# Two batches of attention with float32 products, unnormalised weights and a divisor from ones beside v

## The chip, the core and the metric

The kernel runs on one core of a Trainium2 chip. The core has a matrix engine (TensorE, in the profile PE, with its weight loads as PEld), a vector engine (VectorE, DVE), a scalar engine (ScalarE, ACT), GpSimd (POOL) and SyncE (SP), whose queue starts all transfers here. [...] The metric is the device time of one execution in microseconds, taken as the median of several runs.

## What is computed

```python
# q, k, v: (8 batches, 8 heads, 576 positions, 64)
scores = (q @ k.transpose) / sqrt(64)
mask   = (i // 64) >= (j // 64)          # block causal
scores = where(mask, scores, -1e9) - max(scores)
attn   = exp(scores); attn = attn / (sum(attn) + 1e-9)
x      = (attn @ v), heads side by side: (4608 tokens, 512)
h      = x @ w_in                         # (512, 2048)
g      = h if h >= 1, 0 if h <= -1, else (h + 1)**2 / 4
out    = g @ w_out                        # (2048, 512)
```

All inputs and the output are float32.

## The kernel before

Attention is worked pair by pair: a pair is two heads of one batch, so there are 32 pairs, four to a batch (`Pair`, numbered b and hp). The 576 positions of a head are four full tiles of 128 rows and a last block of 64; the last blocks of both heads share a tile. `attention_steps` walks through the pairs in eight steps each (between two `yield`), and the steps of neighbouring pairs overlap: while pair `cur` is in its first two steps, the products with v of the pair before, `old`, are finished, and in the later steps q and k of the next pair, `nxt`, are loaded, split and transposed.

For each group of rows `scores` makes the scores on PE, their negated maximum on DVE (line 394) and the exponential on ACT (line 398), which also gives the sum of each row; `inverse` adds 1e-9 and takes the reciprocal of that column on DVE (lines 380, 381), and line 404 scales the rows of P in SBUF. `scores_last` does the same for the shared last tile (lines 418 to 430). `turn` and `turn_last` transpose P on PE (line 443, from pair 12 on line 441) into a PSUM bank, and `split` brings it to SBUF: `pa` for the first 256 columns, `pb` for the other 320, `pc` or `pcs` for the last block of keys.

Products in most of the kernel are made in fp32r with a high and a low half: `split` writes the high half on ACT (line 434) and the low half on DVE (line 436), `split_v` does so for v on ACT and POOL (lines 316, 317) into `vsr`, whose 128 columns are the high half in the columns of the head's own 64 and the low half in the other 64. `weighted` multiplies (line 480); its PSUM rows are then two halves to be added, which `add_halves` does through `xtmp` (ACT, line 502; DVE, line 503) into `x32`. `store_x` writes x as a high half (ACT, line 545) and a low half (POOL, line 546) to the rings `xh` and `xl`.

Batch 0 is marked `plain`. There P stays one float32 tile, and v is loaded straight into `vs`, with 64 columns of zeros beside the head's own 64; `both` adds the products of both heads in one bank and writes `xh` and `xl` itself (lines 515, 516). `vs` has one buffer and is loaded anew for each pair.

`work_bank` gives PSUM banks: it alternates between four banks of the feed-forward's output and three work banks until the feed-forward begins, and from then on gives the three alone.

The driver at the end runs the attention's steps. With each it converts pieces of the two weight matrices (`convert`: a transfer, two ACT, three DVE, a POOL, an ACT and a POOL instruction, lines 159 to 182), 64 pieces in all, and from step 36 on (`START`, the middle of pair 4) it takes one step of the feed-forward (`ffn_in`: 12 products a step, lines 626 to 643; `ffn_out`: 12 more, lines 650 and 655) with each step of the attention. What is left of the feed-forward follows when the attention is done. The order in which instructions stand on each engine comes from a scheduler, which starts from this order; each engine then works through its own in that order.

Of the kernel before, what the change touches and what calls it, by code (L numbers as in the profile page):

```python
# [23 lines left out]
def block_attn_then_ffn(  # L24
# [9 lines left out]
    nc = tc.nc  # L34
# [22 lines left out]
    CW = 256  # L57
    F32_TOP = float.fromhex("0x1.dffffcp-96")
    KA = D + NTL
    HOP = 3  # L60

    const = ctx.enter_context(tc.tile_pool(name="const", bufs=1))
# [167 lines left out]
        return moved  # L230


    class Pair:


# [2 lines left out]
        def __init__(self, b, hp):  # L238
            self.b, self.hp = b, hp

            self.plain = b == 0
            self.first = b == 0 and hp == 0

            self.hop = b >= HOP
            self.pr, self.nat = {}, {}

        def load(self, name):
            src = {"q": q, "k": k, "v": v}[name]
            h0 = 2 * self.hp
            if name == "v" and self.plain:  # L250

                self.vs = []
                both = att1.tile([P, 2, NTL + 1, 2, D], F32, tag="pb1", name="vs")
                for j in range(2):
                    vs = both[:, j]
                    nc.gpsimd.memset(vs[:, :, 1 - j, :], 0.0)
                    nc.sync.dma_start(
                        vs[:, :NTL, j, :], src[self.b, h0 + j, :SM, :].rearrange("(t p) d -> p t d", p=P)
                    )
                    nc.sync.dma_start(vs[:BLK, NTL, j, :], src[self.b, h0 + j, SM:, :])  # L260
                    self.vs.append(vs)
                return
            t_ = att2.tile([P, 2 * NTL + 2, D], F32, tag="nat", name=name + "n")
            if name == "v":
                for j in range(2):
                    nc.sync.dma_start(
                        t_[:, j * NTL : (j + 1) * NTL, :],
                        src[self.b, h0 + j, :SM, :].rearrange("(t p) d -> p t d", p=P),
                    )
                nc.sync.dma_start(  # L270
                    t_[:BLK, 2 * NTL :, :],
                    src[self.b, h0 : h0 + 2, SM:, :].rearrange("h p d -> p h d"),
                )
            else:

                nc.sync.dma_start(
                    t_[:, : 2 * NTL, :].rearrange("p (h t) d -> p h (t d)", h=2),
                    src[self.b, h0 : h0 + 2, :SM, :].rearrange("h (p t) d -> p h (t d)", t=NTL),
                )
                for j in range(2):  # L280
                    nc.sync.dma_start(
                        t_[j * BLK : (j + 1) * BLK, 2 * NTL, :], src[self.b, h0 + j, SM:, :]
                    )
            self.nat[name] = t_
# [76 lines left out]
        def begin_b(self):  # L361
            dt, n = (F32, 1) if self.plain else (F32R, 2)
            self.pb = [att1.tile([P, 2, NTL, G1], dt, tag=f"pb{i}", name=f"pb{i}") for i in range(n)]
            self.pc = (
                [att1.tile([BLK, 2, BLK], dt, tag="pa01", name="pc")] if self.plain else pcs
            )
            if not self.plain:
                self.x32 = att1.tile([P, S], F32, tag="x32", name="x32")

        def product(self, ps, j, c0, k0, n, first, last):  # L370
            nc.tensor.matmul(  # L371
# [11 lines left out]
        def scores(self, j, g):  # L383
            tiles = self.GROUPS[g]
            m = len(tiles)
            ps = work_bank("ps_s")
            pr = att3.tile([P, S], F32, tag="pr", name="pr")
            nm = small.tile([P, 2], F32, tag="nm", name="nm")
            sm = small.tile([P, 2], F32, tag="sm", name="sm")
            cols = [slice(at, at + (t + 1) * P) for t, at in tiles]  # L390
            for (t, _), cs in zip(tiles, cols):
                self.product(ps[:, cs], j, t * P, 0, (t + 1) * P, True, True)
            for i, cs in enumerate(cols):
                nc.vector.tensor_reduce(  # L394
                    out=nm[:, i : i + 1], in_=ps[:, cs], axis=AX.X, op=ALU.max, negate=True
                )
            for i, cs in enumerate(cols):
                nc.scalar.activation(  # L398
                    pr[:, cs], ps[:, cs], AF.Exp, bias=nm[:, i : i + 1], scale=1.0,
                    accum_out=sm[:, i : i + 1],  # L400
                )
            self.inverse(sm[:, :m])
            for i, cs in enumerate(cols):
                nc.vector.tensor_scalar_mul(pr[:, cs], pr[:, cs], sm[:, i : i + 1])  # L404
            self.pr[j, g] = as_float32r(pr[:, : cols[-1].stop]) if self.hop else [pr]

        def scores_last(self):

            half = S // 2
            pr = att3.tile([P, S], F32, tag="pr", name="pr")  # L410
            nm = small.tile([P, 3], F32, tag="nm", name="nm")
            sm = small.tile([P, 3], F32, tag="sm", name="sm")
            banks = []
            for i in range(2):
                ps = work_bank("ps_s")
                for j in range(2):
                    self.product(ps[:, :half], j, SM, i * half, half, j == 0, j == 1)
                nc.vector.tensor_reduce(
                    out=nm[:, i : i + 1], in_=ps[:, :half], axis=AX.X, op=ALU.max, negate=True
                )  # L420
                banks.append(ps)
            nc.vector.tensor_tensor(out=nm[:, 2:3], in0=nm[:, 0:1], in1=nm[:, 1:2], op=ALU.min)
            for i in range(2):
                nc.scalar.activation(
                    pr[:, i * half : (i + 1) * half], banks[i][:, :half], AF.Exp,
                    bias=nm[:, 2:3], scale=1.0, accum_out=sm[:, i : i + 1],
                )
            nc.vector.tensor_tensor(out=sm[:, 2:3], in0=sm[:, 0:1], in1=sm[:, 1:2], op=ALU.add)
            self.inverse(sm[:, 2:3])
            nc.vector.tensor_scalar_mul(pr, pr, sm[:, 2:3])  # L430
            self.pr["last"] = as_float32r(pr) if self.hop else [pr]

        def split(self, ps, hi, lo=None):
            nc.scalar.copy(hi, ps)  # L434
            if lo is not None:
                nc.vector.tensor_tensor(out=lo, in0=ps, in1=hi.bitcast(F32), op=ALU.subtract)  # L436
# [36 lines left out]
                ps[:BLK, :P].rearrange("p (h c) -> p h c", h=2), *(x[:BLK] for x in self.pc)  # L473
            )

        def weighted(self, ps, j, parts, first=True, last=True):
            for i, (kt, lo_col, mov) in enumerate(parts):
                vt = self.vs[j][: (BLK if self.plain and kt == NTL else P), kt, :, :]
                for m, x in enumerate(mov):
                    nc.tensor.matmul(  # L480
                        ps[:, lo_col:], vt, x,
                        start=first and i == 0 and m == 0,
                        stop=last and i == len(parts) - 1 and m == len(mov) - 1,
                    )

        def parts_first(self, j):
# [17 lines left out]
                out=self.x32[main, c0 : c0 + n], in0=ps[main, :], in1=xtmp[main, :n], op=ALU.add  # L504
            )

        def both(self, c0, parts):

            n = (G0, G1)[c0 > 0]
            ps = work_bank("ps_av")[:, :n]  # L510
            for j in range(2):
                self.weighted(ps, j, parts(j), j == 0, j == 1)
            at = self.b * S + c0
            hi = xh[:, self.hp, at : at + n]
            nc.scalar.copy(hi, ps)
            nc.vector.tensor_tensor(  # L516
                out=xl[:, self.hp, at : at + n], in0=ps, in1=hi.bitcast(F32), op=ALU.subtract
            )

        def attn_v_first(self):  # L520
            if self.plain:
                return self.both(0, self.parts_first)
            ps = work_bank("ps_av")
            for j in range(2):
                self.weighted(ps[:, j * G0 : (j + 1) * G0], j, self.parts_first(j))
            for j in range(2):
                self.add_halves(ps[:, j * G0 : (j + 1) * G0], j, 0)

        def attn_v(self, j):
            if self.plain:  # L530
                return self.both(G0, self.parts) if j else None
            ps = work_bank("ps_av")[:, :G1]
            self.weighted(ps, j, self.parts(j))
            self.add_halves(ps, j, G0)

        def store_x(self):

            if self.plain:
                return
            c0 = 0  # L540
            while c0 < S:
                at = (self.b * S + c0) % RING
# [9 lines left out]
    def attention_steps():  # L552
# [11 lines left out]
        for i, cur in enumerate(pairs + [None]):  # L564
            nxt = pairs[i + 1] if i + 1 < len(pairs) else None
            if cur:
                cur.scores(0, 0)
                cur.turned(False, 1)
                cur.load("v")
            if old:  # L570
                old.turn(1, 2)
            yield
# [3 lines left out]
            if old:  # L576
                old.attn_v(1)
                old.store_x()
            if not cur:
                return  # L580
            yield
# [159 lines left out]
```

## Time and profile before

| | |
|---|---|
| median of 3 runs | 1286.38 us |
| lowest, highest | 1285.29, 1288.21 us |
| the profiled execution | 1285.23 us |
| its span, first to last instruction | 1283.5 us |
| mean granted TensorE clock | 0.983 |
| HBM read, written | 120.59 MB, 17.83 MB |

A line of the profile names the line of the kernel, the engine, the operation, the tiles that it writes and reads with their shapes, the count, and then busy time, mean duration and idle time of the engine before it. Where two stretches of time are compared, a row gives the length, each engine's busy time with its count of instructions, the granted clock of TensorE (1.00 is full), and what the transfers did. Rows of a timeline give the start and the length. A wide instruction and the next on the same engine overlap a little in these records, so the busy time of an engine is less than the sum of its durations.

### The profile page before, as it was taken

Reading aid. Unit: us, or ns where it says so; the run is one execution under the profiler, and the core shown is the slowest. Engines: PE = TensorE matmul, PEld = TensorE weight load, DVE = VectorE, ACT = ScalarE, POOL = GpSimd, SP = SyncE. Lnnn points to the kernel's source line nnn. Section 1 sums busy time; section 2 is a strip of 40 time slices with the busy share of each in tenths; the row PEclk is TensorE's granted clock in tenths of the full one; section 3 lists DMA queues with packets and bytes.
Section 4 is the critical chain, followed back from the end, with each engine's and each line's share of the span. In section 5 each row is a group of like instructions: output and inputs, shape, how many; then the busy total and the mean of one; then the engine's idle time right before and its main releaser. Section 6 shows DMA issues by size and latency. Waiting matters only on the chain.

```text
span 1283.5 us, 20410 instructions
## 1 busy us (share of the span) xinstructions
PE 1207.2 (94%) x6496; PEld 1018.7 (79%) x6496; DVE 888.4 (69%) x2204; ACT 766.3 (60%) x1855; POOL 472.2 (37%) x466
## 2 busy tenths in 40 slices
PE   5877787899999999999999999999999999999998
PEld 4666665688888888888888888888888888888886
DVE  8998999877677777677777777777777767322222
ACT  6878676666666666666666666666666655322222
POOL 3545766633333333333333333333333332222222
PEclk9889999999999999999999999999999999999999
DMA  5656555434333545555444644464545443333432
GB/s 152 175 151 180 170 186 177 145 125 140 97 106 111 189 143 153 160 159 178 147 155 154 187 137 152 153 189 148 159 146 186 156 142 120 115 99 99 132 99 99
DMA packets 136812, 188.44 MB, mean 147 GB/s; under 512 B 61040, under 2 KB 87664, under 8 KB 136704
## 3 DMA queue, kind: packets, MB, share of 16 engines
q1 hardware_dynamic: 136704, 187.13, 47.2%
q8 instruction: 52, 0.85, 0.3%
q14 instruction: 56, 0.46, 0.1%
HBM read 120.59 MB, written 17.83 MB: 108 GB/s over the span
## 4 chain that ended last, share of the span: by engine, by line
PE 70%; DVE 13%; ACT 8%; issue 4%; DMA 2%; POOL 1%; SPq 1%; ACTq 0%; POOLq 0%; DVEq 0%
PE ph L626 26%; PE po L650 16%; PE po L655 8%; PE ps_av L480 7%; PE ps_s L371 3%; PE ps_s L374 3%; ACT pr L398 3%; PE ps_t L441 3%; PE ps_qk L327 2%; DVE pr L404 2%; ACT qb L331 2%; DVE nm L394 2%; DVE work L169 1%; PE ps_t L443 1%; DVE work L172 1%
## 5 line engine op out<-in xcount | busy, mean ns | idle before, releaser
L641 POOL TENSOR_TENSOR gl<-t,gh 128x512 fp32r<-128x512 f32 x144 | 187.2, 1300 | 577.5 <-ACT gh L640 310.8
L650 PE MATMUL po<-wo,gh 128*128 128x512 f32 x1152 | 299.7, 403 | 0.1
L650 PEld LDWEIGHTS po<-wo,gh 128*128 128x128 f32 x1152 | 210.6, 190 | 40.3 <-ACT gh L640 0.6
L626 PE MATMUL ph<-xh,wih 128*128 128x512 f32 x576 | 238.2, 414 | 1.7 <-DVE t L639 1.7
L636 DVE SCALAR_TENSOR_TENSOR t<-t 128x512 f32<-128x512 f32 x144 | 112.9, 784 | 183.1 <-ACT t L635 181.0
L626 PE MATMUL ph<-xl,wih 128*128 128x512 f32 x576 | 227.4, 395 | 1.1 <-DVE xl L516 1.1
L626 PE MATMUL ph<-xh,wil 128*128 128x512 f32 x576 | 227.9, 396 | 0.0
L635 ACT ACTIVATE t<-ph 128x512 f32<-128x512 f32 x144 | 86.0, 597 | 155.2 <-PE ph L626 155.2
L398 ACT ACTIVATE pr<-ps_s,nm 128x128 f32<-128x128 f32 (+3 forms) x256 | 134.2, 529 | 63.1 <-DVE nm L394 62.8
L655 PE MATMUL po<-wo,gl 128*128 128x512 f32 x576 | 155.4, 391 | 0.0
L394 DVE TENSOR_REDUCE nm<-ps_s 128x1 f32<-128x128 f32 (+3 forms) x256 | 123.6, 485 | 45.2 <-PE ps_s L374 43.6
L371 PE MATMUL ps_s<-ka,qa 68*128 68x288 f32 (+4 forms) x384 | 123.6, 336 | 20.5 <-ACT pr L398 12.8
L640 ACT CAST gh<-t 128x512 fp32r<-128x512 f32 x144 | 90.0, 625 | 84.6 <-DVE t L639 83.0
L626 PEld LDWEIGHTS ph<-xh,wil 128*128 128x128 f32 x576 | 109.4, 190 | 24.5
L434 ACT CAST pb<-ps_t 128x512 fp32r<-128x512 f32 (+1 forms) x140 | 77.5, 553 | 84.8 <-PE ps_t L441 65.5
L317 POOL TENSOR_TENSOR vsr<-vn,vsr 128x256 fp32r<-128x256 f32 (+1 forms) x112 | 82.9, 750 | 119.9 <-ACT vsr L316 119.9
L655 PEld LDWEIGHTS po<-wo,gl 128*128 128x128 f32 x576 | 108.4, 188 | 23.4
L626 PEld LDWEIGHTS ph<-xl,wih 128*128 128x128 f32 x576 | 109.9, 191 | 20.4 <-DVE xl L516 1.4
L626 PEld LDWEIGHTS ph<-xh,wih 128*128 128x128 f32 x576 | 109.4, 190 | 20.3 <-DVE t L639 2.0
L374 PE MATMUL ps_s<-kb,qb 128*128 128x288 f32 (+4 forms) x384 | 121.8, 323 | 0.0
L436 DVE TENSOR_TENSOR pb<-ps_t,pb 128x512 fp32r<-128x512 f32 (+1 forms) x140 | 88.1, 629 | 40.5 <-ACT pb L434 40.5
L404 DVE TENSOR_SCALAR pr<-pr,sm 128x128 f32<-128x128 f32 (+3 forms) x256 | 110.3, 451 | 3.6
(95 smaller groups left out, 2039.1 us busy)
## 6 DMA issues: line engine op xcount, KB each, us to landing
wo<-wo_split SPq DMA_DIRECT2D x144, 512.0 KB, 3.4
prr<-pr SPq DMA_DIRECT2D x80, 192.0 KB, 2.6
prr<-pr SPq DMA_DIRECT2D x60, 256.0 KB, 2.4
out_dram<-ob SPq DMA_DIRECT2D x36, 256.0 KB, 4.0
qn<-in_q_dram SPq DMA_DIRECT2D x32, 256.0 KB, 2.9
kn<-in_k_dram SPq DMA_DIRECT2D x32, 256.0 KB, 3.0
bits<-in_moe_w_in_dram SPq DMA_DIRECT2D x32, 256.0 KB, 3.1
bits<-in_moe_w_out_dram SPq DMA_DIRECT2D x32, 256.0 KB, 3.1
```

The source lines that it names most:

```text
L371: nc.tensor.matmul(ps, qa[:KA, j, c0 : c0 + P], ka[:KA, j, k0 : k0 + n], start=first, stop=False)
L374: nc.tensor.matmul(ps, qb[:, j, c0 : c0 + P], kb[:, j, k0 : k0 + n], start=False, stop=last)
L394: nc.vector.tensor_reduce(out=nm[:, i : i + 1], in_=ps[:, cs], axis=AX.X, op=ALU.max, negate=True)
L398: nc.scalar.activation(pr[:, cs], ps[:, cs], AF.Exp, bias=nm[:, i : i + 1], scale=1.0, accum_out=sm[:, i : i + 1],)
L404: nc.vector.tensor_scalar_mul(pr[:, cs], pr[:, cs], sm[:, i : i + 1])
L480: nc.tensor.matmul(ps[:, lo_col:], vt, x, start=first and i == 0 and m == 0, stop=last and i == len(parts) - 1 and m == len(mov) - 1,)
L626: nc.tensor.matmul(ph, w[:, cc, fs], x[:, cc, xs], start=(cc == 0 and i == 0), stop=(cc == NCC - 1 and i == 2),)
L636: nc.vector.scalar_tensor_tensor(out=t_, in0=t_, scalar=1.0, in1=t_, op0=ALU.min, op1=ALU.mult)
L640: nc.scalar.copy(gh, t_)
L641: nc.gpsimd.tensor_tensor(out=gl, in0=t_, in1=gh.bitcast(F32), op=ALU.subtract)
L650: nc.tensor.matmul(po[tt], gh[:, ts_], wo[:, w, :], start=(fc == 0 and w == 0), stop=False)
L655: nc.tensor.matmul(po[tt], gl[:, ts_], wo[:, 0, :], start=False, stop=fc == NFC - 1)
```

## The change

`PLAIN = 2` makes the first two batches plain, pairs 0 to 7. For them P is no longer scaled: `scores` and `scores_last` leave out the sums, the inverse and the scaling. `vs` is made once, with ones in the 64 columns beside the head's own, and each pair's transfers overwrite the head's columns; `pc` is made once too, with zeros in its lower 64 rows. A product with `vs` then has the weighted v in 64 rows of PSUM and the sum of the weights in the other 64, which `divided` uses: ACT moves the sums, plus 1e-9, to the partitions of the weighted v (into a tile of `xtmp`), DVE takes their reciprocal and multiplies into `x32`. `store_x` now runs for plain pairs as well. `split` copies P for plain pairs on DVE where the tile has more than two dimensions (`pb`, `pc`), no longer on ACT. `both` is gone. v of a plain pair is loaded in the second step of the pair, after the preceding pair's last products, no longer in the first.

```diff
+    PLAIN = 2
...
+    plain = {}
...
-            self.plain = b == 0
+            self.plain = b < PLAIN
...
             if name == "v" and self.plain:
-                self.vs = []
-                both = att1.tile([P, 2, NTL + 1, 2, D], F32, tag="pb1", name="vs")
-                for j in range(2):
-                    vs = both[:, j]
-                    nc.gpsimd.memset(vs[:, :, 1 - j, :], 0.0)
+                if not plain:
+                    both = att1.tile([P, 2, NTL + 1, 2, D], F32, tag="pb1", name="vs")
+                    nc.gpsimd.memset(both[:, 0, :, 1, :], 1.0)
+                    nc.gpsimd.memset(both[:, 1, :, 0, :], 1.0)
+                    nc.gpsimd.memset(both[BLK:, :, NTL, :, :], 0.0)
+                    plain["vs"] = [both[:, j] for j in range(2)]
+                    pc = att1.tile([P, 2, BLK], F32, tag="pa01", name="pc")
+                    nc.gpsimd.memset(pc[BLK:], 0.0)
+                    plain["pc"] = [pc]
+                self.vs, self.pc = plain["vs"], plain["pc"]
+                for j, vs in enumerate(self.vs):
                     nc.sync.dma_start(
...
                 nc.scalar.activation(
                     pr[:, cs], ps[:, cs], AF.Exp, bias=nm[:, i : i + 1], scale=1.0,
-                    accum_out=sm[:, i : i + 1],
-                )
-            self.inverse(sm[:, :m])
-            for i, cs in enumerate(cols):
-                nc.vector.tensor_scalar_mul(pr[:, cs], pr[:, cs], sm[:, i : i + 1])
+                    accum_out=None if self.plain else sm[:, i : i + 1],
+                )
+            if not self.plain:
+                self.inverse(sm[:, :m])
+                for i, cs in enumerate(cols):
+                    nc.vector.tensor_scalar_mul(pr[:, cs], pr[:, cs], sm[:, i : i + 1])
...
         def split(self, ps, hi, lo=None):
+            if lo is None and ps.shape[1:] == hi.shape[1:] and len(ps.shape) > 2:
+                nc.vector.tensor_copy(hi, ps)
+                return
             nc.scalar.copy(hi, ps)
...
-        def both(self, c0, parts):
...
+        def divided(self, ps, heads, c0):
+            n = ps.shape[1] // len(heads)
+            total = att1.tile([P, G1], F32, tag="xtmp", name="xtmp")
+            halves = [slice(j * D, (j + 1) * D) for j in range(2)]
+            for i, j in enumerate(heads):
+                nc.scalar.activation(
+                    total[halves[j], :n], ps[halves[1 - j], i * n : (i + 1) * n], AF.Identity,
+                    bias=EPS, scale=1.0,
+                )
+            rows_ = slice(heads[0] * D, (heads[-1] + 1) * D)
+            nc.vector.reciprocal(total[rows_, :n], total[rows_, :n])
+            for i, j in enumerate(heads):
+                nc.vector.tensor_tensor(
+                    out=self.x32[halves[j], c0 : c0 + n], in0=ps[halves[j], i * n : (i + 1) * n],
+                    in1=total[halves[j], :n], op=ALU.mult,
+                )
...
         def attn_v_first(self):
-            if self.plain:
-                return self.both(0, self.parts_first)
             ps = work_bank("ps_av")
             for j in range(2):
                 self.weighted(ps[:, j * G0 : (j + 1) * G0], j, self.parts_first(j))
+            if self.plain:
+                return self.divided(ps, (0, 1), 0)
...
         def attn_v(self, j):
-            if self.plain:
-                return self.both(G0, self.parts) if j else None
             ps = work_bank("ps_av")[:, :G1]
             self.weighted(ps, j, self.parts(j))
-            self.add_halves(ps, j, G0)
+            self.divided(ps, (j,), G0) if self.plain else self.add_halves(ps, j, G0)
...
         def store_x(self):
-            if self.plain:
-                return
...
                 cur.turned(False, 1)
-                cur.load("v")
+                if not cur.plain:
+                    cur.load("v")
...
                 old.attn_v(1)
                 old.store_x()
+            if cur and cur.plain:
+                cur.load("v")
```

More of the change, by code (lines that the diff above doesn't have):

```diff
@@ L260, in load @@
                     nc.sync.dma_start(vs[:BLK, NTL, j, :], src[self.b, h0 + j, SM:, :])
-                    self.vs.append(vs)
                 return
@@ L363, in begin_b @@
             self.pb = [att1.tile([P, 2, NTL, G1], dt, tag=f"pb{i}", name=f"pb{i}") for i in range(n)]
-            self.pc = (
-                [att1.tile([BLK, 2, BLK], dt, tag="pa01", name="pc")] if self.plain else pcs
-            )
             if not self.plain:
-                self.x32 = att1.tile([P, S], F32, tag="x32", name="x32")
+                self.pc = pcs
+            self.x32 = att1.tile([P, S], F32, tag="x32", name="x32")
         def product(self, ps, j, c0, k0, n, first, last):
@@ L425, in scores_last @@
                     pr[:, i * half : (i + 1) * half], banks[i][:, :half], AF.Exp,
-                    bias=nm[:, 2:3], scale=1.0, accum_out=sm[:, i : i + 1],
-                )
-            nc.vector.tensor_tensor(out=sm[:, 2:3], in0=sm[:, 0:1], in1=sm[:, 1:2], op=ALU.add)
-            self.inverse(sm[:, 2:3])
-            nc.vector.tensor_scalar_mul(pr, pr, sm[:, 2:3])
+                    bias=nm[:, 2:3], scale=1.0,
+                    accum_out=None if self.plain else sm[:, i : i + 1],
+                )
+            if not self.plain:
+                nc.vector.tensor_tensor(out=sm[:, 2:3], in0=sm[:, 0:1], in1=sm[:, 1:2], op=ALU.add)
+                self.inverse(sm[:, 2:3])
+                nc.vector.tensor_scalar_mul(pr, pr, sm[:, 2:3])
             self.pr["last"] = as_float32r(pr) if self.hop else [pr]
         def split(self, ps, hi, lo=None):
+            if lo is None and ps.shape[1:] == hi.shape[1:] and len(ps.shape) > 2:
+                nc.vector.tensor_copy(hi, ps)
+                return
             nc.scalar.copy(hi, ps)
@@ L474, in turn_last, with weighted @@
             )
-        def weighted(self, ps, j, parts, first=True, last=True):
+        def weighted(self, ps, j, parts):
             for i, (kt, lo_col, mov) in enumerate(parts):
-                vt = self.vs[j][: (BLK if self.plain and kt == NTL else P), kt, :, :]
+                vt = self.vs[j][:, kt, :, :]
                 for m, x in enumerate(mov):
@@ L481, in weighted @@
                         ps[:, lo_col:], vt, x,
-                        start=first and i == 0 and m == 0,
-                        stop=last and i == len(parts) - 1 and m == len(mov) - 1,
+                        start=i == 0 and m == 0,
+                        stop=i == len(parts) - 1 and m == len(mov) - 1,
                     )
@@ L505, in add_halves @@
             )
-        def both(self, c0, parts):
[L509 to L518, printed above, removed]
+        def divided(self, ps, heads, c0):
[14 more added lines that the diff above has]
+                )
         def attn_v_first(self):
-            if self.plain:
-                return self.both(0, self.parts_first)
             ps = work_bank("ps_av")
```

## The prediction

> **What bounds the kernel now.** I read the page first, for the span and for which engine is full when.
>
> ```profile
> span 1283.5 us, 20410 instructions
> PE 1207.2 (94%) x6496; PEld 1018.7 (79%) x6496; DVE 888.4 (69%) x2204; ACT 766.3 (60%) x1855; POOL 472.2 (37%) x466
> ...
> PE   5877787899999999999999999999999999999998
> ...
> DVE  8998999877677777677777777777777767322222
> ```
>
> One slice is 32 us. PE is full from the ninth slice on; in the first eight it is not, and there DVE is the fuller engine. The second view, busy time of each engine by stretch, puts numbers to it (columns: length, then PE, PEld, DVE, ACT, POOL busy, granted clock, DMA):
>
> ```profile
> 0.00:112.00 112.00, 81.75 (x426) 65.32 (x427) 98.01 (x293) 86.28 (x240) 52.72 (x73) 0.92 0.57 164
> 112.00:262.00 150.00, 115.84 (x567) 93.38 (x566) 137.38 (x313) 102.81 (x276) 96.81 (x109) 0.92 0.53 168
> 262.00:300.00 38.00, 37.64 (x215) 32.49 (x215) 27.67 (x71) 24.27 (x57) 11.79 (x12) 1.00 0.41 124
> 300.00:1283.00 983.00, 971.96 (x5292) 827.53 (x5291) 625.37 (x1531) 552.98 (x1286) 310.86 (x274) 1.00 0.46 143
> ```
>
> Call them A, B and C (C is the last two). In A DVE is busy 88% and in B 92%, with PE at 73% and 77%; in C PE is at 99% and DVE at 64%. So before 262 us a microsecond of DVE work is worth close to a microsecond, and after it only PE work counts. Which pairs lie where is read from the timeline of DVE: line 430 runs once per pair of heads, in its fourth step.
>
> ```profile
> 27.16 0.51 DVE L430 TENSOR_SCALAR pr<-pr,sm 128x576 f32<-128x576 f32 x1
> ...
> 119.20 0.52 DVE L430 TENSOR_SCALAR pr<-pr,sm 128x576 f32<-128x576 f32 x1
> ...
> 262.55 0.52 DVE L430 TENSOR_SCALAR pr<-pr,sm 128x576 f32<-128x576 f32 x1
> ...
> 568.82 0.52 DVE L430 TENSOR_SCALAR pr<-pr,sm 128x576 f32<-128x576 f32 x1
> 602.42 0.52 DVE L430 TENSOR_SCALAR pr<-pr,sm 128x576 f32<-128x576 f32 x1
> ```
>
> Pairs 0 to 3 (batch 0) take (119.20 - 27.16) / 4 = 23.0 us each and are stretch A. Pairs 4 to 6 take (262.55 - 119.20) / 3 = 47.8 us each, with the feed-forward and most of the weight conversion beside them: B. Pair 7, the last of batch 1, has its products with v in C, where a pair takes 33.6 us. The change touches exactly pairs 0 to 7.
>
> **The change part by part.** DVE first. Line 404 by stretch (length, DVE busy and count, clock, DMA) in A and in B:
>
> ```profile
> 0.00:112.00 112.00, 21.60 (x35) 0.92 0.57 164
> 112.00:262.00 150.00, 17.44 (x25) 0.92 0.53 168
> ```
>
> One undisturbed call of it in DVE's timeline (start, length):
>
> ```profile
> 124.35 0.41 DVE L404 TENSOR_SCALAR pr<-pr,sm 128x384 f32<-128x384 f32 x1
> ```
>
> And the groups by line and shape (busy time, mean ns of one, idle before), line 381 over the whole run, the others in 0 to 262 us:
>
> ```profile
> L381 DVE RECIPROCAL sm<-sm 128x1 f32<-128x1 f32 x160 | 25.0, 156 | 2.8
> L381 DVE RECIPROCAL sm<-sm 128x2 f32<-128x2 f32 x64 | 10.4, 163 | 1.7
> ...
> L380 DVE TENSOR_SCALAR sm<-sm 128x1 f32<-128x1 f32 x37 | 5.3, 143 | 1.3 <-ACT pr L398 1.2
> L380 DVE TENSOR_SCALAR sm<-sm 128x2 f32<-128x2 f32 x15 | 2.4, 157 | 0.1
> L428 DVE TENSOR_TENSOR sm<-sm 128x1 f32<-128x1 f32 x8 | 1.4, 173 | 0.9 <-ACT pr L424 0.9
> L430 DVE TENSOR_SCALAR pr<-pr,sm 128x576 f32<-128x576 f32 x7 | 3.7, 531 | 0.1
> L436 DVE TENSOR_TENSOR pb<-ps_t,pb 128x512 fp32r<-128x512 f32 x9 | 6.1, 681 | 1.6 <-ACT pb L434 1.6
> L436 DVE TENSOR_TENSOR pb<-ps_t,pb 128x384 fp32r<-128x384 f32 x7 | 3.8, 547 | 0.0
> L436 DVE TENSOR_TENSOR pa<-ps_t,pa 128x384 fp32r<-128x384 f32 x7 | 3.8, 548 | 0.7 <-ACT pa L434 0.7
> L436 DVE TENSOR_TENSOR pcs<-ps_t,pcs 64x128 fp32r<-64x128 f32 x3 | 0.8, 276 | 0.0
> L503 DVE TENSOR_TENSOR x<-ps_av,xtmp 64x320 f32<-64x320 f32 x6 | 2.9, 483 | 0.4 <-ACT xtmp L502 0.3
> L503 DVE TENSOR_TENSOR x<-ps_av,xtmp 64x256 f32<-64x256 f32 x6 | 2.5, 420 | 2.8 <-ACT xtmp L502 2.8
> L516 DVE TENSOR_TENSOR xl<-ps_av,xh 128x320 fp32r<-128x320 f32 x4 | 1.9, 481 | 0.0
> L516 DVE TENSOR_TENSOR xl<-ps_av,xh 128x256 fp32r<-128x256 f32 x4 | 1.7, 420 | 1.0 <-ACT xh L515 1.0
> ```
>
> In that timeline an instruction starts about 0.07 us before the one ahead of it has its end, so I take 0.07 off each.
>
> Removed per pair, in both batches: eight scalings (L404), seven adds and seven reciprocals of a column or two (L380, L381), one sum (L428), one scaling (L430). L404 costs 21.60 / 35 = 0.62 us in A, 17.44 / 25 = 0.70 in B: 4.9 and 5.6 us for eight. The others are 5 x 0.143 + 2 x 0.157 + 5 x 0.156 + 2 x 0.163 + 0.17 + 0.53 = 2.8 us. Batch 0 also loses two L516 (0.90). Sum for A: 8.6 us in 26 instructions, less 1.8, is 6.8 us. Batch 1 loses instead the low halves of P (L436: 2 x 0.548 + 2 x 0.547 + 3 x 0.681 + 0.276 = 4.5) and the adding of halves (L503: 2 x 0.483 + 2 x 0.420 = 1.8). Sum for B: 14.7 us in 36 instructions, less 2.5, is 12.2 us.
>
> Added per pair, the same in both: the copies of P out of PSUM into pb and pc go from ACT to DVE. The nearest rows are L436's of the same shapes, which read the same PSUM: 2 x 0.547 + 3 x 0.681 + 0.276 = 3.4 us. Four multiplications by the inverse have L503's shapes: 1.8 us. And three reciprocals of whole tiles, one of 128x256 and two of 64x320. The trace has no reciprocal wider than two columns. From below it costs what another DVE instruction of that length costs (L503): 0.42 + 2 x 0.48 = 1.4 us. From above, L381's one extra column costs 163 - 156 = 7 ns over several dozen calls each, so 0.156 + 255 x 0.007 = 1.9 us and 0.156 + 319 x 0.007 = 2.4 us, together 6.7 us. Against this slope: L380, an add, shows 14 ns from one column to two, and an add of 256 columns certainly doesn't cost 3.6 us (L516 subtracts that many in 0.42). [...] But L380's rows hold waits (its neighbours L404 do), L381's hardly vary, so I take the slope: 6.7 us. Added: 3.4 + 1.8 + 6.7 less 13 x 0.07 = 11.0 us, or 5.7 us by the lower bound.
>
> [...]
>
> Net on DVE per pair: A +4.2 us (lower bound -1.1), B -1.2 us (lower bound -6.5).
>
> How much of L404's saving is real? Undisturbed, 384 columns took 0.41 us; the average over shapes was 0.62 and 0.70. [...] The excess is about 0.2 x 8 = 1.7 us in A and 0.3 x 8 = 2.4 in B; between none and all of it passed on I take half: A +5.1, B 0.0.
>
> What gives time back: DVE is idle 14 of 112 us in A, 2.9 us of a pair's 23.0, and 12.6 of 150 in B, 4.0 us of 47.8. Part of that is the chain from the exponential over add, reciprocal and scaling to the transposes, which now goes from ACT to PE at once; and ACT loses the reading of ten sums, and six copies of some 0.5 us:
>
> ```profile
> L434 ACT COPY pb<-ps_t 128x512 f32<-128x512 f32 x12 | 7.1, 594 | 4.0 <-PE ps_t L443 4.0
> ...
> L545 ACT CAST xh<-x 128x576 fp32r<-128x576 f32 x3 | 2.0, 674 | 1.9 <-DVE x L503 1.9
> L546 POOL TENSOR_TENSOR xl<-x,xh 128x576 fp32r<-128x576 f32 x3 | 5.0, 1668 | 0.0
> ```
>
> Batch 0 pays ACT 0.7 us (L545) and POOL 1.7 us (L546) per pair for storing x, and saves two memsets of v on POOL; batch 1 saves the splitting of v on both. POOL is busy 47% of A and 65% of B, and ACT ends up lighter, so I cost these at nothing; were POOL full, L546 would cost its 1.7 us. Of the idle time I take 1.8 us a pair as regained in A and 1.5 in B. So A: (5.1 - 1.8) x 4 = +13 us. B: -1.5 x 3 = -4.5 us.
>
> PE: batch 1's products go from two fp32r matmuls to one float32, which the trace shows as two instructions too, but longer. One head's eight (first start to the start of what follows), at full clock:
>
> ```profile
> 84.39 2.21 PE L480 MATMUL ps_av<-pb,vs 128*128 128x320 f32 x8
> 86.52 0.43 PE L480 MATMUL ps_av<-pc,vs 64*128 64x64 f32 x2
> ...
> 284.84 1.31 PE L480 MATMUL ps_av<-pb,vsr 128*128 128x320 f32 x8
> 285.98 0.33 PE L480 MATMUL ps_av<-pcs,vsr 128*128 128x64 f32 x2
> ```
>
> 2.13 us against 1.14. Two heads lose 2.0 us; the pa and pc products, 768 + 128 columns beside 2304, scale to another 0.7. For pairs 4 to 6 these 2.7 us hide in PE's 23% idle time of B (uncovered, 8 us over three pairs). For pair 7 they fall into C and count: +2.7 us. Batch 0's products stay float32 and equal in number.
>
> The load of v, four transfers a pair on SP's queue, moves behind the preceding pair's last products. It had to wait for them before as well, since v had one buffer in batch 0; in batch 1 a queue entry may stand for the wait, with the conversion's loads, q, k and the moves into qa and ka behind it. v is needed five steps later, 5/8 of a pair or 14 us even in A. Cost: none, up to 1 us a pair if the loads of weights behind it come late.
>
> Sum: +13 - 4.5 + 2.7 = +11 us on the span of 1283.5, so 1294.7; the profiled execution had 1285.2 in all, 1.7 above its span, and the median of the runs is 1.1 above that: **1297 us**. By the bounds of this case, A from +5 (all idle time regained) to +24 (all blocking passed on, none regained), B from -16 to +4: 1281 to 1317, with its middle half between 1290 and 1305.
>
> **The rivals.**
>
> *The wide reciprocal is cheap* (faster). If a column costs about a cycle, A is -1.1 and B -6.5 us a pair: 4 x -1.1 + 3 x -6.5 + 2.7 = -21 us, less half of the blocking passed on (+0.9 x 4 + 1.2 x 3 = +7): 1272 us, or 1265 without that. For it speaks only that two columns don't prove a slope; against it, the 7 ns.
>
> [...]
>
> *The held bank* (slower still). In B only three banks serve scores, transposes and products with v. A bank of ps_av is now held over ACT's move, a 2.4 us reciprocal and the multiplication, and PE waits for a bank already:
>
> ```profile
> PE ps_s L371 <- ACT pr L398: 12.1, 3, 4.5
> ```
>
> If each of the three holds a pair delays PE by the reciprocal's length, 6.7 us x 3 pairs = +20 us: 1317 us. It decides as soon as PE meets a full set of banks within 2 us of a product; with DVE as the bound most of it would be hidden.
>
> **How the numbers follow.** Forecast 57%, cheap reciprocal 18%, chain 14%, held bank 11%. Within 0.2% of 1286.4 (2.6 us either way) a measurement of this kernel can't tell it from no change; its runs spread by 2.9 us. Faster: the cheap reciprocal's 18, 9 of the chain's 14 and 2 of the forecast's low end: 0.29. Same: 0.06. Slower: 0.65. The range runs from the cheap reciprocal's lower figure to the held bank's, 1265 to 1317; the forecast's own range is 1281 to 1317.
>
> **What would show it.** Right: a RECIPROCAL of 64x320 near 2.4 us and of 128x256 near 1.9; the period of pairs 0 to 3 near 26 us, of pairs 4 to 6 near 46; DVE still above 88% busy up to the point where PE fills; that point about 8 us later; pb's copies on DVE at 0.55 to 0.68 us. Wrong: a reciprocal under 0.6 us; or periods that fall although DVE's work per pair in A has grown; or PE idle for ps_av's release.

## The result, and the profile after

The changed kernel takes 1302.53 us in the median (1301.56 to 1303.99), against 1285.84 beside it: a ratio of 1.013, interval 1.0109 to 1.0151. The forecast was 1297, the direction and the range held, and 11 us of slowing were forecast where 17 came. The profiled execution took 1301.57 us:

```profile
span 1299.5 us, 20144 instructions
PE 1219.2 (94%) x6496; PEld 1023.0 (79%) x6496; DVE 892.4 (69%) x2060; ACT 747.2 (57%) x1723; POOL 460.0 (35%) x450
...
PE   6777788799999999999999999999999999999998
...
DVE  7889989868777777777777777776777777322222
```

DVE runs 144 instructions fewer and yet is busy 4 us longer; PE is full from the ninth slice on, as before, and a slice is now 32.5 us long instead of 32.1. To see where the time went, I cut both executions at the same places of the work: at the first maximum over 288 columns of a pair (it opens the pair's fourth step) for pairs 0, 4, 7 and 8. In the timeline of DVE of the changed kernel these marks are:

```profile
18.18 0.94 DVE L427 TENSOR_REDUCE nm<-ps_s 128x1 f32<-128x288 f32 x2
...
128.68 0.45 DVE L427 TENSOR_REDUCE nm<-ps_s 128x1 f32<-128x288 f32 x1
...
272.23 0.81 DVE L427 TENSOR_REDUCE nm<-ps_s 128x1 f32<-128x288 f32 x2
309.81 0.82 DVE L427 TENSOR_REDUCE nm<-ps_s 128x1 f32<-128x288 f32 x2
```

Between the marks lie stretch A (four pairs), B (three pairs beside the feed-forward and the conversion) and pair 7. The view of busy time by stretch (length, then PE, PEld, DVE, ACT, POOL, granted clock, transfers), first the kernel before:

```profile
19.90:114.20 94.30, 75.52 (x404) 60.14 (x404) 84.81 (x252) 77.58 (x221) 50.52 (x63) 0.91 0.59 174
114.20:259.40 145.20, 111.47 (x545) 89.77 (x544) 133.82 (x305) 99.64 (x268) 92.17 (x106) 0.92 0.53 166
259.40:293.30 33.90, 33.54 (x186) 28.70 (x186) 24.34 (x64) 21.43 (x51) 13.04 (x12) 0.98 0.39 121
```

and the changed kernel:

```profile
18.20:128.70 110.50, 79.93 (x394) 60.47 (x394) 96.91 (x191) 71.84 (x165) 42.64 (x52) 0.80 0.48 145
128.70:272.20 143.50, 115.82 (x550) 91.21 (x550) 127.77 (x242) 89.47 (x209) 88.05 (x100) 0.93 0.56 173
272.20:309.80 37.60, 37.49 (x195) 31.36 (x194) 25.65 (x51) 18.09 (x38) 11.88 (x10) 0.96 0.36 107
```

A is 16.2 us longer, B 1.7 shorter, pair 7 3.7 longer; it began 1.7 earlier, which makes +16.5 at the last mark and +16.0 at the end. In A DVE's work grew by 12.1 us (3.0 a pair), with 61 instructions fewer, and its idle time from 9.5 to 13.6. The new groups of DVE in the first 300 us, by line and shape (count, busy time, mean ns, idle time before), say what the work is:

```profile
L533 DVE RECIPROCAL xtmp<-xtmp 64x320 f32<-64x320 f32 x15 | 32.2, 2145 | 4.7 <-ACT xtmp L528 4.5
L446 DVE COPY pb<-ps_t 128x512 f32<-128x512 f32 x24 | 16.2, 677 | 0.0
L533 DVE RECIPROCAL xtmp<-xtmp 128x256 f32<-128x256 f32 x8 | 14.0, 1749 | 5.9 <-ACT xtmp L528 5.9
L446 DVE COPY pb<-ps_t 128x384 f32<-128x384 f32 x16 | 8.6, 535 | 5.1 <-PE ps_t L457 5.1
L535 DVE TENSOR_TENSOR x<-ps_av,xtmp 64x320 f32<-64x320 f32 x15 | 7.3, 484 | 0.3
L446 DVE COPY pc<-ps_t 64x128 f32<-64x128 f32 x8 | 2.2, 273 | 0.0
L535 DVE TENSOR_TENSOR x<-ps_av,xtmp 64x256 f32<-64x256 f32 x16 | 6.7, 417 | 0.2
```

The wide reciprocals are the dear ones: 2 x 2.145 + 1.749 = 6.0 us a pair, and (2145 - 1749) / 64 = 6.2 ns for each further column.

### The profile page after: what moved, and what is told of

Same layout as the page of the kernel before. It is cut to its first block, busy times and chain, and to the rows that moved or that the text cites. A ratio compares the mean times of both kernels' runs of the same rounds, so it can differ in the third digit from the quotient of the medians.

```text
span 1299.5 us, 20144 instructions
## 1 busy us (share of the span) xinstructions
PE 1219.2 (94%) x6496; PEld 1023.0 (79%) x6496; DVE 892.4 (69%) x2060; ACT 747.2 (57%) x1723; POOL 460.0 (35%) x450
## 4 chain that ended last, share of the span: by engine, by line
PE 67%; DVE 7%; ACT 4%; issue 2%; DMA 1%; POOL 0%; ACTq 0%; POOLq 0%
PE ph L645 25%; PE po L669 16%; PE po L674 8%; PE ps_av L494 7%; PE ps_s L382 3%; PE ps_s L379 3%; PE ps_t L455 3%; PE ps_qk L337 2%; ACT pr L406 2%; ACT qb L341 1%; DVE pr L413 1%; DVE sm L388 1%; DMA prr<-pr 1%; PE ps_t L457 1%; DVE nm L402 1%
## 5 line engine op out<-in xcount | busy, mean ns | idle before, releaser
L448 ACT CAST pb<-ps_t 128x512 fp32r<-128x512 f32 (+1 forms) x120 | 66.5, 555 | 81.3 <-PE ps_t L455 66.5
L327 POOL TENSOR_TENSOR vsr<-vn,vsr 128x256 fp32r<-128x256 f32 (+1 forms) x96 | 73.1, 772 | 106.8 <-ACT vsr L326 106.8
L450 DVE TENSOR_TENSOR pb<-ps_t,pb 128x512 fp32r<-128x512 f32 (+1 forms) x120 | 75.4, 629 | 37.5 <-ACT pb L448 37.3
L658 DVE TENSOR_TENSOR t<-ph,t 128x512 f32<-128x512 f32 x144 | 98.4, 684 | 2.1
```

The costliest lines, as they stand in the source:

```text
L658: nc.vector.tensor_tensor(out=t_, in0=ph, in1=t_, op=ALU.max)
```

## The experiments

Eleven kernels ran. Those sent together share the runs of the kernel before, whose median was 1286.38 us for the first four, 1285.01 for the next four and 1286.55 for the last three.

**The reciprocal left out.** This kernel leaves out the reciprocal of line 533, so it multiplies x by the sum. From the changed kernel:

```diff
             rows_ = slice(heads[0] * D, (heads[-1] + 1) * D)
-            nc.vector.reciprocal(total[rows_, :n], total[rows_, :n])
```

> The changed kernel without the wide reciprocal of line 533; x is multiplied by the sum where it should be divided. Theory (DVE's work sets the pace of pairs 0 to 6, and the reciprocals, 2 x 2.15 + 1.75 = 6.0 us a pair, are what the change adds): pairs 0 to 3 come from 27.6 us to about 22, pairs 4 to 6 from 47.8 to 44 at most; together 20 to 33 us less than 1302.5, so 1270 to 1282, below the kernel before. Rival (the move of the copies to DVE and the chain over ACT, DVE and PE cost as much as the reciprocals): less than 12 us gained, 1291 or more, still above the kernel before.

Measured: 1275.22 us, 0.9922 of the kernel before (0.9904 to 0.9940). By stretch, A and B:

```profile
18.90:105.70 86.80, 70.18 (x396) 56.58 (x394) 76.73 (x185) 67.54 (x158) 47.80 (x53) 0.92 0.57 165
105.70:248.30 142.60, 116.90 (x548) 92.28 (x548) 116.62 (x227) 89.92 (x214) 88.55 (x100) 0.93 0.60 186
```

The reader should set these beside the changed kernel's. In A 20.2 us of DVE work left and 23.7 us of time; the granted clock rose from 0.80 to 0.92. In B 11.2 us of DVE work left and 0.9 of time. So the theory holds for A, and more than holds; in B nearly nothing came of it: pairs 4 to 6 take 47.5 us each, where the theory said 44 at most.

**The reciprocal run twice.**

```diff
             nc.vector.reciprocal(total[rows_, :n], total[rows_, :n])
+            nc.vector.reciprocal(total[rows_, :n], total[rows_, :n])
```

> The changed kernel with the wide reciprocal run twice, so that x is multiplied by the sum. Theory (in pairs 0 to 3 a microsecond of DVE costs one of time; without the reciprocals they fell from 27.6 to 21.7 us): pairs 0 to 3 go to 33 to 34 us each, +24 us, and pairs 4 to 6 add up to 6 each: 1325 to 1345. Rival (without the reciprocals another engine had become the bound or the gain was in the chain, so the cost is not linear): under 1320 or over 1350.

Measured: 1329.53 us, 1.0340 (1.0314 to 1.0366). None, one and two runs of each reciprocal give 1275.2, 1302.5 and 1329.5: 27.3 and 27.0 us a step. A and B:

```profile
18.10:148.50 130.40, 88.48 (x397) 67.69 (x396) 117.93 (x203) 71.82 (x165) 44.85 (x51) 0.71 0.42 127
148.50:299.60 151.10, 123.65 (x557) 96.74 (x558) 140.66 (x247) 89.12 (x208) 89.48 (x100) 0.87 0.51 159
```

A grew by 19.9 us with 21.0 of DVE work. B, which had gained 0.9 us by losing 11 us of DVE work, lost 7.6 by gaining 13: it has a floor near 140 us that DVE reaches only from some 130 us of work on.

**The copies on ACT again.**

```diff
             if lo is None and ps.shape[1:] == hi.shape[1:] and len(ps.shape) > 2:
-                nc.vector.tensor_copy(hi, ps)
+                nc.scalar.copy(hi, ps)
                 return
```

> The changed kernel with the copies of pb and pc on ACT again. They take 3.0 us of DVE a pair and would take some 2.6 of ACT. Theory (DVE's work sets the pace): pairs 0 to 3 gain 2 to 3 us each and pairs 4 to 6 1 to 3, together 11 to 20 us: 1283 to 1292. Rival (ACT's chain is as tight as DVE, so that the move costs nothing either way): 1299 to 1306.

Measured: 1287.51 us, 1.0017 (0.9998 to 1.0035), as the theory's figure, with an unusual spread of 1283.6 to 1292.3 over ten runs. The profiled execution was at the upper end of it:

```profile
18.50:126.40 107.90, 79.86 (x395) 63.37 (x394) 88.50 (x170) 80.54 (x191) 45.64 (x53) 0.81 0.50 150
126.40:265.40 139.00, 116.53 (x552) 91.74 (x553) 120.95 (x221) 95.31 (x226) 87.82 (x98) 0.94 0.57 176
```

In this execution the gain lies elsewhere than expected: 8.4 us of DVE work left A for 2.6 us of time, so here A isn't bound by DVE's work alone (it is idle 18%), and B gained 4.5. Why ACT's copies give A so much idle time isn't settled; ACT itself was busy 75%.

**One batch the new way.** Batch 0 alone:

```diff
-    PLAIN = 2
+    PLAIN = 1
```

> The changed kernel with one batch treated the new way, not two. Theory (batch 0 pays nearly all of it, as the two traces' periods say: +14.5 us by pair 4, -1.6 over pairs 4 to 6, +3 at pair 7): batch 0 alone costs 14 to 16 us, so 1299 to 1303. Rival (batch 1's longer float32 products are what costs): 1286 to 1293.

Measured: 1311.3 us, 1.0199 (1.0177 to 1.0220). This missed: batch 0 alone costs 25 us, 9 more than both batches together, so batch 1 the new way is a gain. A and B:

```profile
18.80:133.60 114.80, 83.83 (x397) 63.62 (x396) 99.06 (x199) 73.31 (x173) 46.85 (x56) 0.78 0.48 143
133.60:284.20 150.60, 117.40 (x549) 94.65 (x549) 137.84 (x314) 100.34 (x267) 95.91 (x109) 0.85 0.51 160
```

Batch 0's cost reaches past its own four pairs: A is 20.5 us longer than before, and B, whose pairs are worked as before, 5.4 longer, with 4.0 us more DVE work. Of the 5.4 us, 4.8 lie in pair 4 alone (51.4 us against 46.6), at a granted clock of 0.77 against 0.93: TensorE runs at half its clock there from 127.1 to 147.5 us, across the mark at 133.6. So the 1.7 us that the changed kernel shows as won in B would be a difference of two, if the two add: 5.4 lost to what batch 0 left over, 7.1 won by batch 1.

**The converse: batch 0 as before, batch 1 the new way.** The old loading of v, the old scaling, the copies on ACT and `both` are kept for batch 0:

```diff
+            self.ones = b == 1
...
-            if not self.plain:
+            if not self.ones:
                 self.inverse(sm[:, :m])
...
         def attn_v(self, j):
+            if self.plain and not self.ones:
+                return self.both(G0, self.parts) if j else None
```

> Batch 0 as in the kernel before, batch 1 the new way. With the new way for batch 0 alone the time was 1311, for both 1302.5, so if the two add up, batch 1's part is -9 us: 1275 to 1280 (theory: batch 0's cost is DVE's work in the stretch that DVE bounds, batch 1's gain is work taken off DVE and POOL beside the feed-forward). Rival (batch 1's way costs nothing or something by itself and only mends what batch 0's left behind): 1284 to 1292.

Measured: 1278.61 us, 0.9946 (0.9927 to 0.9965). The two halves add up: +24.9 and -6.4 make +18.5, where both together gave +16.7. A and B:

```profile
20.30:115.80 95.50, 75.39 (x396) 60.52 (x394) 87.09 (x250) 76.63 (x213) 50.24 (x65) 0.87 0.58 173
115.80:253.60 137.80, 115.11 (x555) 91.86 (x556) 122.76 (x226) 88.73 (x206) 82.28 (x94) 0.95 0.56 174
```

A is as before within 1.2 us and B 7.4 shorter.

**The old float32 scheme for two batches**, without ones and without wide reciprocals, from the kernel before:

```diff
-            self.plain = b == 0
+            self.plain = b < 2
```

> The kernel before with its own float32 scheme (scaled P, zeros beside v, both heads in one bank) for two batches, not one: the float32 products of batch 1 alone, without ones and without the wide reciprocal. Theory: DVE loses in batch 1 lines 436 and 503 and gains line 516, 4.5 + 1.8 - 0.9 us less overlaps, about 4.7 us a pair, over pairs 4 to 6 up to 14 us; PE's longer products of pair 7 cost 3 us: 1273 to 1281. Rival (the float32 products hold PE up in pairs 4 to 6, 2.7 us each): 1285 or more.

Measured: 1279.95 us, 0.9962 (0.9947 to 0.9976). B took 138.3 us:

```profile
113.50:251.80 138.30, 119.53 (x558) 93.86 (x557) 111.55 (x271) 91.91 (x247) 82.06 (x101) 0.91 0.58 178
```

DVE has 11 us less to do here than in the run before this one and B is no shorter: the floor again. What batch 1 gains comes with the float32 product itself, with no halves to split, subtract and add; whether the ones have a part in it, these two intervals, which overlap, don't show.

**Two buffers for the sums.**

```diff
-            total = att1.tile([P, G1], F32, tag="xtmp", name="xtmp")
+            turn_["n"] += 1
+            total = att1.tile([P, G1], F32, tag=("xtmp", "pa11")[turn_["n"] % 2], name="xtmp")
```

> The changed kernel with two buffers in turn for the tile of sums, so that ACT's move for one product need not wait for the multiplication of the last. Theory (the length of the reciprocals on DVE costs, not the chain through one buffer): 1299 to 1306, as the changed kernel. Rival (the chain ACT, reciprocal, multiplication through one buffer makes the idle time that grew from 2.4 to 3.4 us a pair): 1292 to 1297.

Measured: 1302.47 us, 1.0143 (1.0107 to 1.0178), the changed kernel's own time. The wait for the single buffer isn't what costs.

**One reciprocal for both heads.** The first head's product is made beside the second's, and both sums stand in one tile:

```diff
+        def divided_both(self):
...
+            for j in range(2):
+                ps = work_bank("ps_av")[:, :G1]
+                self.weighted(ps, j, self.parts(j))
+                nc.scalar.activation(
+                    total[halves[j], :], ps[halves[1 - j], :], AF.Identity, bias=EPS, scale=1.0
+                )
+                pss.append(ps)
+            nc.vector.reciprocal(total, total)
```

> The changed kernel with one reciprocal of 128x320 for both heads in place of two of 64x320 (the first head's product is made in the step of the second's). Theory (cost by columns, whatever the partitions): 2.1 us of DVE less a pair, pairs 0 to 3 at 25.5 us, in all 8 to 13 us less than 1302.5: 1289 to 1295. Rival (a reciprocal of 128 rows takes longer than one of 64, or the later first product costs as much as it saves): 1298 or more.

Measured: 1286.35 us, 1.0010 (0.9995 to 1.0025), a larger gain than expected. The reciprocal (its group, and A by stretch):

```profile
L552 DVE RECIPROCAL xtmp<-xtmp 128x320 f32<-128x320 f32 x7 | 15.0, 2146 | 1.8 <-ACT xtmp L548 1.7
```

```profile
17.80:114.10 96.30, 73.97 (x399) 59.10 (x398) 86.95 (x190) 70.59 (x163) 44.16 (x51) 0.86 0.56 166
```

128 rows take 2146 ns and 64 took 2145: the cost goes by columns. A lost 10.0 us of DVE work and 14.2 of time; the other 4.2 are idle time of DVE (13.6 to 9.3). The time that reciprocals waited for ACT's move fell from 8.3 us to 4.0.

**Combinations.** Three kernels: the converse with one reciprocal for both heads; the same with batch 1's copies on ACT; and both batches the new way with one reciprocal and the copies on ACT. Their edits are those shown.

> Batch 0 as in the kernel before, batch 1 the new way with one reciprocal for both heads. Theory: batch 1 lies where DVE isn't the only bound; the second reciprocal's removal brought 1.0 us over pairs 4 to 6 and 1.7 at pair 7 when both batches had it, so 2 to 4 us below 1278.6: 1273 to 1278. Rival (it is worth as much as in batch 0, 3.6 us a pair): 1262 to 1269.

> As the kernel with batch 0 as before and batch 1 the new way with one reciprocal, with batch 1's copies on ACT besides. With both batches the new way this brought 4.5 us over pairs 4 to 6 and 1.9 at pair 7: 1268 to 1274. Rival (with the reciprocal gone DVE has room, and the copies cost ACT what they cost DVE): 1273 to 1280.

> Both batches the new way, with one reciprocal for both heads and the copies on ACT. If the two edits add up (-16 and -15 of 1302.5): 1270 to 1275. Rival (both free the same idle DVE time in pairs 0 to 3, where the copies alone brought 0.7 us a pair): 1278 to 1285.

Measured: 1282.57 (0.9970, 0.9955 to 0.9985), 1282.58 (0.9965, 0.9951 to 0.9980) and 1278.96 (0.9935, 0.9915 to 0.9955). The first two miss on the slow side, outside the ranges of their theories and of their rivals: less DVE work in B brings nothing there. The first one's B:

```profile
116.60:255.50 138.90, 116.67 (x543) 93.37 (x544) 112.66 (x224) 87.80 (x207) 81.96 (x95) 0.91 0.56 177
```

10.1 us of DVE work less than in the converse alone, and 1.1 us longer. The third lies in the range of its rival: its edits bring 23.6 us together, not the 31 of their sum, and its A and B are

```profile
18.10:111.50 93.40, 74.71 (x401) 61.29 (x399) 82.37 (x174) 80.83 (x192) 48.32 (x56) 0.84 0.59 177
111.50:248.20 136.70, 115.08 (x540) 91.31 (x540) 110.36 (x210) 93.18 (x225) 86.14 (x97) 0.93 0.59 181
```

Both the converse (0.9946) and this kernel (0.9935) are a little faster than the kernel before, and so is the old scheme for two batches (0.9962); the three intervals overlap.

## Why the prediction held, point by point

*DVE bounds A and B.* Right for A in that time follows DVE's work there from 76.7 us of it (86.8 long) over 84.8 (94.3), 96.9 (110.5) to 117.9 (130.4), and in all runs but one it is 7 to 16 us above it. The exception is the changed kernel with its copies on ACT. Only half right for B: from 134 us of DVE work on it is 145 to 151 us long, but between 108 and 123 us it stays between 137 and 143. That "a microsecond of DVE work is worth close to a microsecond" was read off a busy share of 92%, and the share doesn't tell how near the next limit is. What sets the floor was not tried; in the runs on it PE is busy 114 to 120 us at a granted clock of 0.90 to 0.95.

*The wide reciprocal.* Shown. The step from one column to two gave 7 ns a column and 6.7 us a pair; measured are 6.2 ns and 6.0 us. The cheap-reciprocal rival was wrong by its first condition. That L380's rows hold waits isn't shown: in the first 262 us of the kernel before its 52 instructions took 126 to 170 ns each, L381's 52 took 142 to 168.

*Copies and multiplications.* By the rows chosen for them 3.4 and 1.8 us; measured 2 x 0.535 + 3 x 0.677 + 0.273 = 3.4 and 2 x 0.484 + 2 x 0.417 = 1.8.

*Blocking half passed on.* Too much, it seems: DVE's work in A grew by 3.0 us a pair, and the sum with the measured reciprocals and nothing passed on is 4.2 - 0.7 = 3.5. No run shows that what L404 takes beyond its undisturbed time (0.41 us for 384 columns) is passed on to other instructions: the conversion's three DVE lines (L166, L169, L172; in the changed kernel L167, L170, L173) took 0.46 us an instruction in A before (32.8 us for 71) and 0.47 after (31.7 for 67), in B 0.54 (61.0 for 114) and 0.50 (59.7 for 120).

*"Of the idle time I take 1.8 us a pair as regained in A."* This is the step that failed. DVE's idle time in A grew instead, 9.5 to 13.6 us. The trace puts part of it down to reciprocals that wait for ACT's move of the sums, right behind PE's product. Waits of DVE in A of the changed kernel (total us, times, longest):

```profile
DVE xtmp L533 <- ACT xtmp L528: 8.3, 8, 1.6
DVE pb L446 <- PE ps_t L457: 4.9, 2, 2.8
```

A second buffer left the time as it was and one reciprocal fewer shortened the idle time, so it isn't the tile; it may be the order on DVE's queue, where a reciprocal stands ahead of work that could run. That was not tried.

The traces show a second path that bears on this idle time. Three times in A, once a pair from the second on, PE's queue comes to products of x with w_in, the feed-forward's first, which need the x of the pair before. That x now comes by way of ACT's move, the reciprocal, the multiplication and `store_x`, and PE stands still for it (again total us, times, longest):

```profile
PE ph L645 <- ACT xh L561: 7.3, 3, 2.4
```

With 2.9 us more for `xl`, which POOL writes, that is 10.2 us in A; it was 1.1 in the kernel before, none without the reciprocals and 12.7 with two, so storing x, which the forecast cost at nothing, is on a path that PE waits on. Within 2.5 us of the end of each of the three waits for `xh`, TensorE's granted clock falls to half for 10.2 us (at 49.7, 77.0 and 104.3 us). In all runs whose clock in A averages 0.84 or less, DVE is idle 11 to 19 us there, in the others 7 to 10. That would make PE a partner in the growth, but the order of cause and effect is not shown: inside the changed kernel's A, DVE is idle 8% of the half-clock time and 15% of the rest. A run with those products later in PE's queue would tell; there is none.

With work and idle time together A came to (110.5 - 94.3) / 4 = 4.05 us a pair, against the forecast's 3.3.

*B -4.5 us.* The trace's -1.7 hides a mechanism that the forecast lacked: batch 0's slowing goes on in B (+5.4 with batch 0 alone), and batch 1's gain was larger than forecast (7.4 us in B in the converse run). That the whole came out within 6 us is partly luck: two sizes were both set too low, against each other, batch 0's cost (13 us in the forecast, 25 by itself) and batch 1's gain (2 us net, against 6 by itself).

*Pair 7 +2.7 us.* The products with v took PE 4.00 us in this stretch before and 6.08 in the changed kernel: +2.1. The stretch itself grew by 3.7, of which another 1.1 are the feed-forward's products with w_in (49 in 13.7 us against 48 in 12.6, at clocks of 0.96 and 0.98). With products with v of the same length, the stretch is 34.7 us long in the converse, where 44 products with w_in fall into it, and 35.7 in the changed kernel with its copies on ACT. So the term was right in kind and a little too high, and the 3.7 are not its measure.

*The load of v, the held bank.* Neither was tried by itself. PE was idle for the release of a bank of ps_av, one of the forecast's signs of being wrong: 10.0 us in the first 300 of the changed kernel, against 4.9 before. The kernel with one reciprocal holds two banks at once over a reciprocal. There PE waited 17.0 us for them, and yet it is faster in A and no slower in B (142.6 us), so the held bank isn't what decides here. None of the products waited for a transfer of v: what PE's products from `vs` waited for, in the first 300 us of the changed kernel (us, times; "issue" is time in which PE waited for nothing that the profile shows), is

```profile
  issue: 5.3, 27
  ACT pa L448: 4.4, 4
  DVE pb L446: 0.2, 1
```

*The other signs and the range.* The reciprocals came out at 2.15 and 1.75 us for 2.4 and 1.9, the periods at 27.6 and 47.8 us for 26 and 46, and DVE's busy share at 88% in A and 89% in B. The range's lower end doesn't follow from its own terms: A at (4.2 - 2.9) x 4 = +5 and B at (-1.2 - 4.0) x 3 = -16, with all idle time regained and none of L404's excess passed on, give 1278 and not 1281; DVE's idle time in A grew, from 9.5 to 13.6 us, and in B, from 11.4 to 15.7.

## What to carry to other kernels

Dividing after the product trades many cheap scalings for few wide reciprocals. Here these cost 27 us, and no kernel with them was measurably faster than the old scheme for two batches without them. Keep the sums on partitions, where a reciprocal is one column wide (156 ns here), or fill all 128 rows of one instruction before a second is issued, which took 16 us off. Here the step between one column and two priced an operation of 320 columns to within 12%; test such a price by leaving the operation out and by doubling it. Where a change treats two stages at once, run each alone: in the trace of both, one stage's delay and the other's gain partly cancelled.

## What the runs showed of the hardware

A reciprocal on DVE took 156 ns for one column, 1749 for 256 and 2145 for 320, and as long for 128 rows as for 64. TensorE's granted clock in A fell with the pace: 0.92 without the reciprocals, 0.80 with one, 0.71 with two, at nearly the same PE work of 394 to 397 matmuls, whose busy time rose from 70.2 over 79.9 to 88.5 us. In these three runs PE, which was not full, became slower as DVE had more to do.

Taken in slices of 0.1 us, the granted clock in A is full or half, but for the slices in which it changes. In the changed kernel it is at half for 44.7 us of A, in stretches of 6.8, 6.8, 10.2, 10.2 and 10.2 us and one that runs on over the mark; before, for 17.0 us (6.8, 6.8, 3.4); without the reciprocals, for four stretches of 3.4. What makes it fall is not shown: in the 3.4 us before each of the six falls in A of the changed kernel PE was busy for 0.85 to 2.2 us.
